# Attention and SwiGLU on one core: where buffers begin, when the next batch is loaded, and where attention products stand

## The chip, the core and the metric

The kernel runs on one core of one Trainium2 chip. The core has a matrix engine (PE, with its weight loads shown as PEld), a vector engine (DVE), a scalar engine (ACT), GpSimd (POOL) and SP, which here only issues DMAs. The metric is the device time of one execution in microseconds. The kernel before was run three times: 1498.76, 1501.85 and 1501.93 us, median 1501.85. A further execution was taken with the profiler.

## What is computed

Two stages follow one another, for four batches of 12416 tokens with 128 channels:

```python
h = mab(I, x)                      # 32 inducing rows attend to all tokens of a batch
a = mab(x, h)                      # each token attends to the 32 rows of h
g, val = a @ w_gate, a @ w_val     # 128 -> 1536
out = (g / (1 + exp(-g)) * val) @ w_out    # 1536 -> 128

def mab(q, kv):
    s = scale * (q @ kv.T); s = exp(s - s.max(-1)); return (s / (s.sum(-1) + 1e-9)) @ kv
```

All inputs and the output are float32, and the large products are made from a rounded part (`hi`) and a remainder (`lo`).

## The kernel before

**Columns, tiles and slots.** The tokens of a batch are cut into 25 columns. The first has 512 tokens, the next twelve have 512 each, the last twelve 480 each. A column is worked through in 12 tiles of the hidden width, so a batch has 300 slots, 12 to a column. In each slot `front` makes two products from the buffer `stack` of the column (gate, L668, and value, L669), ACT computes silu (L671) and DVE the product h (L676). One slot later `split` rounds h to `h_hi` (L685, mostly ACT) and takes the remainder `h_lo` (L687, POOL, on DVE in three tiles of twelve). Some slots later `back` adds three products to the accumulator of the column (L701 and L702 from `h_hi`, L703 from `h_lo`). The first column of batch 0 has one unsplit product instead (L699). After the twelfth tile, `evac` copies the accumulator to `ob` (L710, DVE) and SP writes it out (L712).

**The order.** It is written out by hand: each engine runs its instructions in the order in which the program issues them. The list `pend` holds split tiles that wait for `back`. `ahead`, the number of tiles in front and pend together, grows by a sixth each slot up to 10 while the attention of the next batch runs, and falls back to 5.

**Attention beside the columns.** While a batch's columns run, the steps of the next batch's attention are issued between `front` and `back`, each from the slot that `plan` gives it: `load_xt` (L225), `s1` and `max_b` (first scores, their maximum), `hacc` (the sum over tokens), `h_c`, `s2` (second scores), `exp2`, and `proj_round` (the weights `tw` of the batch). `PA` holds the slots for batch 1 (beside batch 0), `PB` those for batches 2 and 3. `clear` moves a step off the slots that `TABU` bars (slot 5 of each column, in `PA` only). The steps s1, max_b, hacc, h_c and s2 take a buffer of `ps_o`, which has two and also holds the column's accumulator.

**From attention to a column.** `post` makes the next group of columns from the second scores: sum, reciprocal and norm, transpose `aT`, then `a_hi` (L457, a copy on DVE that rounds; once on ACT at the start), `a_lo` (L462, POOL) and `spread` (L478), whose DMAs copy both into `stack`, 12 slots apart for each column.

**Loads.** The buffers `xt_sb` are four. Batch 0 reads its last four chunks of x from them by slots 50, 54, 60 and 66, and the loads of batch 1 go into the same buffers in that order. SP issues its DMAs in the order of the program, and one that has to wait for its buffer holds all that come after it.

**Where buffers begin.** The pools lie one behind another in each partition. Adding up their tiles, the three `stack` buffers begin at 160 bytes modulo 256, the eleven `h_hi` and ten `h_lo` at 32, and the weights that these products load (`tw`, `wo_hi`, `wo_lo`) at 224. A buffer of 512 columns has 2048 bytes, so all of a pool begin alike.

Of the kernel before, what the change touches and what calls it, by code (L numbers as in the profile page):

```python
# [9 lines left out]
F32 = mybir.dt.float32  # L10
# [22 lines left out]
NF = len(FC)  # L33
W = 32 * max(CH)
WF = 32 * max(FC)
NT = DFF // P
SCALE = 1.0 / math.sqrt(C)

# [62 lines left out]
    70: "sb:84:97:1",  # L101
}

PA = dict(LX=(38, 5), S1=(61, 7), MX=7, E1=10, LN=(27, 4), HA=(3, 3, 3), HB=(9, 6), HC=(8, 4), HD=5, H2=6, E2=5, PR=(0, 3), PQ=2, TABU=(5,))
PB = dict(LX=(0, 9), S1=(25, 7), MX=6, E1=9, LN=(28, 4), HA=(3, 3, 3), HB=(9, 3), HC=(8, 4), HD=6, H2=5, E2=5, PR=(0, 3), PQ=1, TABU=())


@with_exitstack
def induced_set_attention_then_swiglu(ctx: ExitStack, tc: tile.TileContext, xt, xn, ind, wgv, wo, out):
# [52 lines left out]
    class Piece:  # L162
# [23 lines left out]
        def add(self):  # L186
            nc.gpsimd.tensor_add(out=self.w.bitcast(I32), in0=self.t.bitcast(I32), in1=self.lw.bitcast(I32))
# [3 lines left out]

        def lo(self):
            nc.gpsimd.tensor_sub(out=wo_lo[:, self.cs], in0=self.w, in1=wo_hi[:, self.cs].bitcast(F32))

    class Batch:
        pass

    def attention(b, one, xn0=None, xt0=None):
# [253 lines left out]
            st.at[q] = sgl.tile([P, WF], F32, name="aT")  # L452
            nc.vector.transpose(out=st.at[q][:, :32 * FC[q]], in_=sl2(*fblocks(q)).rearrange("p t m -> p (t m)"))

        def a_hi(q, eng=nc.vector.tensor_copy):
            st.ah[q] = sgl.tile([P, WF], F32R, name="a_hi")
            eng(out=st.ah[q][:, :32 * FC[q]], in_=st.at[q][:, :32 * FC[q]])  # L457

# [4 lines left out]

        def stack(u):
            if u not in st.stack:
                st.stack[u] = stp.tile([P, WF], F32R, name="stack")
            return st.stack[u]

        def spread(u):
# [19 lines left out]
            nc.vector.tensor_reduce(out=st.zm, in_=st.zps[:, :M * FC[0]].rearrange("p (t m) -> p t m", m=M), op=ALU.max, axis=AX.X)  # L489

        def z2():
            st.z = att.tile([P, FC[0], M], F32, name="z")
            nc.vector.tensor_sub(out=st.z, in0=st.zps[:, :M * FC[0]].rearrange("p (t m) -> p t m", m=M),
                                 in1=st.zm.unsqueeze(2).broadcast_to([P, FC[0], M]))

# [46 lines left out]
    def plan(st, p):  # L542

        f, s = st.f, []

        def add(slot, step, *args):
            s.append((slot, lambda: f[step](*args)))

        def clear(slot):

            while slot % NT in p["TABU"]:
                slot += 1
            return slot

        def blocks(q):
            return CH0[q], CH0[q] + CH[q]

        for q in range(NCH):
            add(p["LX"][0] + p["LX"][1] * q, "load_xt", q)
            add(clear(p["S1"][0] + p["S1"][1] * q), "s1", q)  # L560
        last = clear(p["S1"][0] + p["S1"][1] * (NCH - 1))
        mb = clear(last + p["MX"])
        add(last + 2, "max_a"), add(mb, "max_b")
        e1 = mb + p["E1"]
        for q in range(NXN):
            add(e1 - p["LN"][0] + p["LN"][1] * q, "load_xn", q)
            add(e1, "exp1_part", q)
            add(e1, "eT", q)
            add(e1 + p["HA"][q], "hacc", q, (0, NXN - 1))
        add(e1, "exp1_part", NXN, NCH - 1)  # L570
        for q in range(NXN, NCH):
            at = clear(e1 + p["HB"][0] + p["HB"][1] * (q - NXN))
            add(at - p["HC"][0], "load_xn", q)
            add(at - p["HC"][1], "eT", q)
            add(at, "hacc", q, (q, q))
        add(at, "h_a")
        add(at + 2, "h_b")
        hn = clear(at + p["HD"])
        add(hn, "h_c")
        for i, q in enumerate(S2O):  # L580
            at = clear(hn + 4 + p["H2"] * i)
            add(at, "s2", *blocks(q))
            if i + NXT < NCH:
                add(at + 1, "load_xt", S2O[i + NXT])
            add(at + 1, "s2_max", *blocks(q))
            add(at + 3, "s2_sub", *blocks(q))
        e2 = at + p["E2"]
        add(e2, "exp2")
        st.e1, st.bursts = e1, {e1, e2}
        for i in range(2):  # L590
            add(e2 + p["PR"][i], "proj_round", i)
            for k in range(NG * NG):
                add(e2 + p["PR"][i] + 3 + k * p["PQ"], "proj_spread", i, k // NG, k % NG)
        for q in range(NF):
            first = [u for u, (p, j) in enumerate(COLS) if p == q][0]
            s += post(st, q, nc.gpsimd, SLOTS + NT * (first - NST) + 2, SLOTS)
        return sorted(s, key=lambda x: x[0])
# [60 lines left out]
    def front(st, b, c, t):  # L658
        u = Tile()
        q, j = COLS[c]  # L660
        u.b, u.q, u.j, u.t = b, q, j, t
        n = u.n = WF if q == 0 else 32 * FC[q]

        u.whole = b == 0 and c == 0
        rhs = st.stack[c][:, :n]
        u.g = ps_gv.tile([P, 512], F32, name="gv")
        u.v = ps_gv.tile([P, 512], F32, name="gv")
        nc.tensor.matmul(out=u.g[:, :n], lhsT=st.w[:, wcol(0, t)], rhs=rhs, start=True, stop=True)  # L668
        nc.tensor.matmul(out=u.v[:, :n], lhsT=st.w[:, wcol(1, t)], rhs=rhs, start=True, stop=True)  # L669
        s = sip.tile([P, WF], F32, name="silu")  # L670
        nc.scalar.activation(out=s[:, :n], in_=u.g[:, :n], func=AF.Silu)  # L671
        if u.whole:
            u.h = hip.tile([P, WF], F32, name="h_hi")
        else:
            u.h = u.v if t in DVE_TILES else hp.tile([P, WF], F32, name="h")
        nc.vector.tensor_mul(out=u.h[:, :n], in0=u.v[:, :n], in1=s[:, :n])  # L676
        return u

    def split(u):
        if u.whole:  # L680
            return
        n = u.n
        u.hi = hip.tile([P, WF], F32R, name="h_hi")
        u.lo = lop.tile([P, WF], F32R, name="h_lo")
        (nc.vector.tensor_copy if u.cast_dve else nc.scalar.copy)(out=u.hi[:, :n], in_=u.h[:, :n])  # L685
        eng = nc.vector if u.t in DVE_TILES or u.last else nc.gpsimd
        eng.tensor_sub(out=u.lo[:, :n], in0=u.h[:, :n], in1=u.hi[:, :n].bitcast(F32))  # L687
# [28 lines left out]
    for b in range(B):  # L716
# [12 lines left out]
        for slot in range(SLOTS):  # L729
            c, t = slot // NT, slot % NT  # L730
            u = front(cur, b, c, t)
            u.cast_dve = t in CAST
            u.last = b == B - 1 and slot == SLOTS - 1
            if wait:
                split(wait[0])
                pend.append(wait.pop(0))
            wait.append(u)
            if slot in bursts:
                u.cast_dve = True
                split(u)  # L740
                pend.append(wait.pop(0))
            for a in (cur, nxt):
                while a is not None and a.steps and a.steps[0][0] <= slot:
                    a.steps.pop(0)[1]()
            ahead = min(ahead + 1 / RAMP, HI) if nxt is not None and slot < last_burst else max(ahead - 1 / RAMP, SKEW)
            if slot in bursts:
                ahead = SKEW
            while len(pend) + len(wait) > ahead:
                back(pend.pop(0))
# [44 lines left out]
```

## Time and profile before

| | |
|---|---|
| three runs | 1498.76, 1501.85, 1501.93 us |
| profiled execution | 1499.66 us, of which the span of the instructions is 1497.6 us |
| granted clock of TensorE | 0.999 |
| PE, PEld busy | 1475.7, 1166.2 us |
| ACT, DVE, POOL busy | 1283.6, 1214.6, 1208.5 us |

The span runs from the first to the last instruction; the few microseconds around it belong to the execution too. Matmul rows give a duration that is modelled and longer than the distance to the next one, so a busy PE has to be read by the distances between starts. "[0.70 <-DVE ob]" in a row is idle time of that engine before it, and what ended it. Idle time is counted from the modelled end.

### The profile page before, as it was taken

How to read it: one execution, taken by the hardware profiler on the slowest of the kernel's cores; microseconds unless marked ns; L12 is line 12 of the kernel's file. 1: busy time of each engine (PE TensorE's matmuls, PEld its weight loads, DVE VectorE, ACT ScalarE, POOL GpSimd, SP SyncE). 2: the span in 40 equal slices, each digit the busy share in tenths (PEclk: the TensorE clock that was granted, in tenths of full speed). 3: DMA queues.
4: the chain of work that ended last, by engine and by line, in shares of the span. 5: the costliest groups of instructions: out<-in, count | busy, mean ns of one | idle time of the engine just before them, and what ended most of it. 6: DMA issues, size and time to landing. Idle time of an engine off the chain costs nothing.

```text
span 1497.6 us, 24960 instructions
## 1 busy us (share of the span) xinstructions
PE 1475.7 (99%) x7465; PEld 1166.2 (78%) x7465; DVE 1214.6 (81%) x2083; ACT 1283.6 (86%) x2389; POOL 1208.5 (81%) x995
## 2 busy tenths in 40 slices
PE   8899999999999999999999999999999999999999
PEld 5576777788887776788887777678888887888887
DVE  6788778878888778788888878878878878878877
ACT  5787888789898887889989888789898898898897
POOL 1588767878898778788888877978889888888887
PEclk9999999999999999999999999999999999999999
DMA  9026322221133333121114324221111111111110
GB/s 369 23 94 187 135 96 94 79 61 56 40 109 120 122 125 112 46 67 37 40 44 131 125 87 156 78 69 48 41 40 35 38 41 41 33 41 39 41 40 20
DMA packets 50822, 119.80 MB, mean 80 GB/s; under 512 B 11392, under 2 KB 28288, under 8 KB 50688
## 3 DMA queue, kind: packets, MB, share of 16 engines
q1 hardware_dynamic: 50688, 118.22, 24.6%
q8 instruction: 59, 0.97, 0.3%
q14 instruction: 75, 0.61, 0.1%
HBM read 62.87 MB, written 25.43 MB: 59 GB/s over the span
## 4 chain that ended last, share of the span: by engine, by line
PE 87%; POOL 2%; ACT 2%; DVE 1%; issue 1%; DVEq 0%; ACTq 0%; POOLq 0%
PE o L701 17%; PE o L703 17%; PE o L702 16%; PE gv L668 16%; PE gv L669 16%; PE o L257 2%; POOL h_lo L687 2%; PE o L305 1%; ACT h_hi L685 1%; ACT silu L671 1%; POOL s_all L449 1%; DVE h L676 1%; PE gv L406 0%; ACT s_all L289 0%; DVE ob L710 0%
## 5 line engine op out<-in xcount | busy, mean ns | idle before, releaser
L687 POOL TENSOR_TENSOR h_lo<-h,h_hi 128x512 fp32r<-128x512 f32 (+1 forms) x890 | 1109.5, 1270 | 238.8 <-ACT h_hi L685 186.9
L671 ACT ACTIVATE silu<-gv 128x512 f32<-128x512 f32 (+1 forms) x1200 | 704.4, 588 | 127.0 <-PE gv L668 89.6
L676 DVE TENSOR_TENSOR h<-gv,silu 128x512 f32<-128x512 f32 (+1 forms) x891 | 594.3, 668 | 206.8 <-ACT silu L671 162.3
L685 ACT CAST h_hi<-h 128x512 fp32r<-128x512 f32 (+1 forms) x788 | 475.5, 603 | 54.0 <-DVE h L676 47.6
L668 PE MATMUL gv<-stack,tw 128*128 128x512 f32 (+1 forms) x1200 | 469.3, 391 | 1.3 <-ACT h_hi L685 0.8
L701 PE MATMUL o<-h_hi,wo_lo 128*128 128x512 f32 (+1 forms) x1188 | 464.4, 391 | 3.8 <-DVE ob L710 2.1
L703 PE MATMUL o<-h_lo,wo_hi 128*128 128x512 f32 (+1 forms) x1188 | 463.2, 390 | 0.6
L669 PE MATMUL gv<-stack,tw 128*128 128x512 f32 (+1 forms) x1200 | 461.8, 385 | 1.8 <-DVE h L676 0.6
L702 PE MATMUL o<-h_hi,wo_hi 128*128 128x512 f32 (+1 forms) x1188 | 458.5, 386 | 0.0
L701 PEld LDWEIGHTS o<-h_hi,wo_lo 128*128 128x128 f32 x1188 | 223.0, 188 | 81.9 <-issue 33.9
L669 PEld LDWEIGHTS gv<-stack,tw 128*128 128x128 f32 x1200 | 225.2, 188 | 53.9 <-ACT silu L671 4.8
L668 PEld LDWEIGHTS gv<-stack,tw 128*128 128x128 f32 x1200 | 225.7, 188 | 50.2 <-issue 3.8
L703 PEld LDWEIGHTS o<-h_lo,wo_hi 128*128 128x128 f32 x1188 | 222.4, 187 | 52.6 <-POOL h_lo L687 12.1
L702 PEld LDWEIGHTS o<-h_hi,wo_hi 128*128 128x128 f32 x1188 | 223.2, 188 | 36.8
L676 DVE TENSOR_TENSOR gv<-gv,silu 128x512 f32<-128x512 f32 (+1 forms) x297 | 201.7, 679 | 46.4 <-ACT silu L671 40.7
L687 DVE TENSOR_TENSOR h_lo<-gv,h_hi 128x512 fp32r<-128x512 f32 (+1 forms) x297 | 197.3, 664 | 1.0
L685 ACT CAST h_hi<-gv 128x512 fp32r<-128x512 f32 (+1 forms) x294 | 167.9, 571 | 4.8 <-DVE gv L676 2.5
L710 DVE COPY ob<-o 128x512 f32<-128x512 f32 (+1 forms) x100 | 66.3, 663 | 1.4 <-PE o L703 1.4
L685 DVE CAST h_hi<-h 128x512 fp32r<-128x512 f32 (+1 forms) x103 | 46.1, 448 | 0.0
L462 POOL TENSOR_TENSOR a_lo<-aT,a_hi 128x512 fp32r<-128x512 f32 (+2 forms) x27 | 36.2, 1340 | 1.5 <-ACT a_hi L457 1.5
L433 POOL TENSOR_TENSOR s_all<-s_all,mx 128x448 f32<-128x448 f32 (+3 forms) x28 | 26.9, 961 | 0.7 <-DVE mx L429 0.7
L449 POOL TENSOR_TENSOR s_all<-s_all,sm 128x512 f32<-128x512 f32 (+2 forms) x27 | 25.9, 958 | 0.4 <-DVE sm L445 0.4
(159 smaller groups left out, 497.4 us busy)
## 6 DMA issues: line engine op xcount, KB each, us to landing
xt_sb<-xt SPq DMA_DIRECT2D x32, 896.0 KB, 5.1
xn_sb<-xn SPq DMA_DIRECT2D x18, 896.0 KB, 6.2
out<-ob SPq DMA_DIRECT2D x52, 256.0 KB, 2.0
out<-ob SPq DMA_DIRECT2D x48, 240.0 KB, 2.0
stack<-a_hi SPq DMA_DIRECT2D x96, 64.0 KB, 2.0
stack<-a_lo SPq DMA_DIRECT2D x96, 64.0 KB, 2.0
stack<-a_hi SPq DMA_DIRECT2D x96, 60.0 KB, 2.0
stack<-a_lo SPq DMA_DIRECT2D x96, 60.0 KB, 2.0
```

Source lines behind the costliest of these rows:

```text
L449: eng.tensor_mul(out=a, in0=a, in1=st.sm[q][:, :FC[q]].unsqueeze(2).broadcast_to([P, FC[q], M]))
L462: eng.tensor_sub(out=st.al[q][:, :n], in0=st.at[q][:, :n], in1=st.ah[q][:, :n].bitcast(F32))
L668: nc.tensor.matmul(out=u.g[:, :n], lhsT=st.w[:, wcol(0, t)], rhs=rhs, start=True, stop=True)
L669: nc.tensor.matmul(out=u.v[:, :n], lhsT=st.w[:, wcol(1, t)], rhs=rhs, start=True, stop=True)
L671: nc.scalar.activation(out=s[:, :n], in_=u.g[:, :n], func=AF.Silu)
L676: nc.vector.tensor_mul(out=u.h[:, :n], in0=u.v[:, :n], in1=s[:, :n])
L685: (nc.vector.tensor_copy if u.cast_dve else nc.scalar.copy)(out=u.hi[:, :n], in_=u.h[:, :n])
L687: eng.tensor_sub(out=u.lo[:, :n], in0=u.h[:, :n], in1=u.hi[:, :n].bitcast(F32))
L701: nc.tensor.matmul(out=o[:, :n], lhsT=wo_lo[:, ws], rhs=u.hi[:, :n], start=(t == 0), stop=False)
L702: nc.tensor.matmul(out=o[:, :n], lhsT=wo_hi[:, ws], rhs=u.hi[:, :n], start=False, stop=False)
L703: nc.tensor.matmul(out=o[:, :n], lhsT=wo_hi[:, ws], rhs=u.lo[:, :n], start=False, stop=(t == NT - 1))
L710: nc.vector.tensor_copy(out=ob[:, :n], in_=o[:, :n])
```

## The change

Four things are changed.

1. The buffers of the pools `stp`, `hip` and `lop` get 64 more columns (`WB`), 2304 bytes, so that a column can begin at an offset in them. `AT` gives the offsets in columns of stack, h_hi and h_lo: 16, 48 and 48 for columns of 512 tokens (so 160 + 64 and 32 + 192 bytes, both 224 modulo 256), none for those of 480. The tile z of the start moves from the pool `att` (two buffers) to `sgl` (one), which makes the space. The net shift of the pools behind is a multiple of 256 bytes.
2. The loads of x for batch 1 are issued from slot 51 on, every fifth slot, where they began at 38.
3. `TABU` and `clear` are gone. Instead a step that takes a buffer of `ps_o` is held back, with all steps of its list behind it, while the tile that `back` takes next is the last or the first of a column.
4. `a_hi` in `post` is made by a reduction (maximum over one element) on DVE, where it was a copy.
The start still makes its one a_hi on ACT.

```diff
+WB = WF + 64
+AT = (16, 48, 48), (0, 0, 0)
...
-PA = dict(LX=(38, 5), S1=(61, 7), MX=7, E1=10, LN=(27, 4), HA=(3, 3, 3), HB=(9, 6), HC=(8, 4), HD=5, H2=6, E2=5, PR=(0, 3), PQ=2, TABU=(5,))
-PB = dict(LX=(0, 9), S1=(25, 7), MX=6, E1=9, LN=(28, 4), HA=(3, 3, 3), HB=(9, 3), HC=(8, 4), HD=6, H2=5, E2=5, PR=(0, 3), PQ=1, TABU=())
+PA = dict(LX=(51, 5), S1=(61, 7), MX=7, E1=10, LN=(27, 4), HA=(3, 3, 3), HB=(9, 6), HC=(8, 4), HD=5, H2=6, E2=5, PR=(0, 3), PQ=2)
+PB = dict(LX=(0, 9), S1=(25, 7), MX=6, E1=9, LN=(28, 4), HA=(3, 3, 3), HB=(9, 3), HC=(8, 4), HD=6, H2=5, E2=5, PR=(0, 3), PQ=1)
...
+    def at(u):
+
+        return AT[u > NG * FC.count(max(FC))]
...
-        def a_hi(q, eng=nc.vector.tensor_copy):
+        def same(out, in_):
+            nc.vector.tensor_reduce(out=out, in_=in_.unsqueeze(2), op=ALU.max, axis=AX.X)
+
+        def a_hi(q, eng=same):
...
-                st.stack[u] = stp.tile([P, WF], F32R, name="stack")
+                st.stack[u] = stp.tile([P, WB], F32R, name="stack")[:, at(u)[0]:][:, :WF]
...
-            st.z = att.tile([P, FC[0], M], F32, name="z")
+            st.z = sgl.tile([P, FC[0], M], F32, name="z")
...
         def add(slot, step, *args):
-            s.append((slot, lambda: f[step](*args)))
-
-        def clear(slot):
-
-            while slot % NT in p["TABU"]:
-                slot += 1
-            return slot
+            def go():
+                f[step](*args)
+
+            go.acc = step in ("s1", "max_b", "hacc", "h_c", "s2")
+            s.append((slot, go))
...
-            u.h = hip.tile([P, WF], F32, name="h_hi")
+            u.h = hip.tile([P, WB], F32, name="h_hi")[:, :WF]
...
-        u.hi = hip.tile([P, WF], F32R, name="h_hi")
-        u.lo = lop.tile([P, WF], F32R, name="h_lo")
+        u.hi = hip.tile([P, WB], F32R, name="h_hi")[:, u.at[1]:u.at[1] + WF]
+        u.lo = lop.tile([P, WB], F32R, name="h_lo")[:, u.at[2]:u.at[2] + WF]
...
             for a in (cur, nxt):
                 while a is not None and a.steps and a.steps[0][0] <= slot:
+
+                    if getattr(a.steps[0][1], "acc", False) and pend and pend[0].t in (NT - 1, 0):
+                        break
                     a.steps.pop(0)[1]()
```

The calls of `clear` in `plan` become their arguments.

More of the change, by code (lines that the diff above doesn't have):

```diff
@@ L559, in plan @@
             add(p["LX"][0] + p["LX"][1] * q, "load_xt", q)
-            add(clear(p["S1"][0] + p["S1"][1] * q), "s1", q)
-        last = clear(p["S1"][0] + p["S1"][1] * (NCH - 1))
-        mb = clear(last + p["MX"])
+            add(p["S1"][0] + p["S1"][1] * q, "s1", q)
+        last = p["S1"][0] + p["S1"][1] * (NCH - 1)
+        mb = last + p["MX"]
         add(last + 2, "max_a"), add(mb, "max_b")
@@ L571, in plan @@
         for q in range(NXN, NCH):
-            at = clear(e1 + p["HB"][0] + p["HB"][1] * (q - NXN))
+            at = e1 + p["HB"][0] + p["HB"][1] * (q - NXN)
             add(at - p["HC"][0], "load_xn", q)
@@ L577, in plan @@
         add(at + 2, "h_b")
-        hn = clear(at + p["HD"])
+        hn = at + p["HD"]
         add(hn, "h_c")
         for i, q in enumerate(S2O):
-            at = clear(hn + 4 + p["H2"] * i)
+            at = hn + 4 + p["H2"] * i
             add(at, "s2", *blocks(q))
@@ L661, in front @@
         u.b, u.q, u.j, u.t = b, q, j, t
+        u.at = at(c)
         n = u.n = WF if q == 0 else 32 * FC[q]
```

## The prediction

> **What bounds the kernel now.** I read the page first, then the groups by form, then the timeline of the matrix engine.
>
> ```profile
> span 1497.6 us, 24960 instructions
> PE 1475.7 (99%) x7465; PEld 1166.2 (78%) x7465; DVE 1214.6 (81%) x2083; ACT 1283.6 (86%) x2389; POOL 1208.5 (81%) x995
> PE 87%; POOL 2%; ACT 2%; DVE 1%; issue 1%; DVEq 0%; ACTq 0%; POOLq 0%
> ```
>
> PE is busy 99% of the span and owns 87% of the chain that ended last: this is a PE-bound kernel, and only two things can make it shorter, less time from one matmul to the next, or fewer moments in which PE waits. The busy time hides both, since a matmul of 0.39 us in the rows is followed by the next one after 0.23. So the distance of starts is what has to be read. Two clean stretches of batch 3, first and last row of each, with the count from the windows view (40 and 43 distances):
>
> ```profile
> 1289.79 0.39 PE L668 MATMUL gv<-stack,tw 128*128 128x512 f32 x1
> ...
> 1298.96 0.39 PE L668 MATMUL gv<-stack,tw 128*128 128x512 f32 x1
> 1379.69 0.38 PE L703 MATMUL o<-h_lo,wo_hi 128*128 128x480 f32 x1
> ...
> 1388.97 0.38 PE L701 MATMUL o<-h_hi,wo_lo 128*128 128x480 f32 x1
> 1290.00:1299.00 9.00, 9.00 (x41) 1.00 0.12 29
> 1380.00:1389.00 9.00, 9.00 (x44) 1.00 0.15 48
> ```
>
> 512 columns: 9.17 / 40 = 229.3 ns a matmul. 480 columns: 9.28 / 43 = 215.8 ns. The 32 columns between them cost 13.5 ns, 0.42 ns each, so 512 columns alone are worth 216 ns and some 13 ns are a fixed part, the same in both widths. The granted clock is 1.00 in both.
>
> **The starts of the buffers.** The 512-column matmuls that stream from the buffers that move:
>
> ```profile
> L668 PE MATMUL gv<-stack,tw 128*128 128x512 f32 x624 | 251.8, 404 | 1.3 <-ACT h_hi L685 0.8 <-DVE h L676 0.3
> L701 PE MATMUL o<-h_hi,wo_lo 128*128 128x512 f32 x612 | 246.1, 402 | 3.8 <-DVE ob L710 2.1 <-DVE hn L311 1.7
> L669 PE MATMUL gv<-stack,tw 128*128 128x512 f32 x624 | 244.1, 391 | 1.8 <-DVE h L676 0.6 <-DVE h_hi L676 0.6 <-ACT silu L671 0.4
> L703 PE MATMUL o<-h_lo,wo_hi 128*128 128x512 f32 x612 | 242.2, 396 | 0.0
> L702 PE MATMUL o<-h_hi,wo_hi 128*128 128x512 f32 x612 | 240.2, 392 | 0.0
> ```
>
> That is 2 x 624 + 3 x 612 = 3084, so each nanosecond of distance is 3.1 us of the kernel: no other part of the change has such a lever. No row shows a start at 224. Low end: the whole fixed part goes, 13 x 3084 = -40 us. High end: the slowest distance that these matmuls keep for a round, in the rows below (three rows are left out, so four distances), 0.96 / 4 = 240 ns, 11 ns more, +33 us.
>
> ```profile
> 1301.26 0.41 PE L668 MATMUL gv<-stack,tw 128*128 128x512 f32 x1
> ...
> 1302.22 0.39 PE L703 MATMUL o<-h_lo,wo_hi 128*128 128x512 f32 x1
> ```
>
> I take zero. The nearest rows are the stretches above: L668 and L669 stream from buffers that begin at 160, L701 to L703 from buffers at 32, and both take 0.23 in the clean rows; and a 480-column stream, which ends half a period further on, has the same fixed part. Two starts and two ends give one price, so a third start most likely gives it again. The Trainium skill, page "SBUF — State Buffer", section "Who interferes with whom", lets only the port pair of VectorE and GpSimd contend and says that PE waits for nobody; by it, too, the term is zero. The same skill's "TensorE: Matmul & The Clock Gate", section "Back-to-back issue gap", has N/2.4 + 2.5 ns, 216 ns at 512 columns; by that the term could reach -41 us, an estimate, and the trace stands 13 ns above it at both widths.
>
> **The rounding of a (L457).**
>
> ```profile
> L457 DVE CAST a_hi<-aT 128x512 fp32r<-128x512 f32 x11 | 12.0, 1091 | 0.0
> L457 DVE CAST a_hi<-aT 128x480 fp32r<-128x480 f32 x12 | 11.1, 928 | 0.0
> L441 DVE TENSOR_REDUCE sm<-s_all 128x16 f32<-128x512 f32 x12 | 8.1, 676 | 0.0
> L441 DVE TENSOR_REDUCE sm<-s_all 128x4 f32<-128x128 f32 x3 | 0.8, 276 | 0.0
> L685 DVE CAST h_hi<-h 128x512 fp32r<-128x512 f32 x55 | 25.4, 464 | 0.0
> 103.30 1.52 DVE L457 CAST a_hi<-aT 128x512 fp32r<-128x512 f32 x1
> 105.02 0.44 PE L668 MATMUL gv<-stack,tw 128*128 128x512 f32 x1
> 106.08 0.50 PE L669 MATMUL gv<-stack,tw 128*128 128x512 f32 x1 [0.62 <-DVE h L676]
> 1361.58 1.23 POOL L687 TENSOR_TENSOR h_lo<-h,h_hi 128x480 fp32r<-128x480 f32 x1 [0.19 <-ACT h_hi L685]
> ```
>
> The same cast takes 464 ns as h_hi and 1091 as a_hi, so some 0.6 us of it is waiting, while POOL runs h_lo back to back. A reduction over one element reads as many elements and writes 512 instead of 16; from 4 to 16 outputs the two L441 rows differ by 400 ns for 384 elements, 1.04 ns each, with nothing left over for 12 more outputs. I take 676 ns. The skill's "VectorE: DVE Perf Modes", section "The perf-mode tier table", speaks against the edit: a 32-bit copy runs at twice the rate of a reduction. By it the 23 casts would grow by 676 - 464 = 0.21 us each, 4.9 us of DVE; the L457 row says that this copy does not get its rate here, and decides.
>
> What PE gains: at 103.30 the long cast holds back DVE's product for h, and PE stands 1.06 instead of 0.23 us between L668 and L669: 1.52 - 0.68 = 0.84 us returns. In the other 22 the shorter cast (0.42 or 0.28 us earlier) reaches PE over ACT and POOL; the POOL row shows 0.19 us of idle behind one of them, while POOL is what PE waits for there. Whether each of the 22 shows it I can't say from one row, so I take half, 22 x 0.19 / 2 = 2.0 us (2.1, rounded down). Ends: 0 (DVE is idle 19% of the span) and 22 x 0.35 = 7.7 us. Together **2.8 us**.
>
> **Loads from slot 51.**
>
> ```profile
> 89.31 23.54 SPq L225 DMA_DIRECT2D xt_sb<-xt  x2
> 121.04 0.58 SPq L478 DMA_DIRECT2D stack<-a_lo  x1
> 123.84 0.40 PE L703 MATMUL o<-h_lo,wo_hi 128*128 128x512 f32 x1
> 125.06 0.47 PE L668 MATMUL gv<-stack,tw 128*128 128x512 f32 x1 [0.82 <-ACT h_hi L685]
> DMA to landing us min/median/max: 3.7/4.4/5.6
> xt_sb<-xt SPq DMA_DIRECT2D x32, 896.0 KB, 5.1
> ```
>
> SP sits on the second load of batch 1 until batch 0 has read that buffer, and behind it wait the output DMA and the spread of column 5 (slot 46). Its last part is issued at 121.04 and lands 3.7 us or more later, at 124.7 (the row of landings is that of these four parts), and slot 60's L668, the first reader, starts at 125.06, 1.22 after L703 instead of 0.23: 0.99 us. The row names ACT, but a wait for several is put down to the last one. With first loads at 51, 56, 61 and 66 the buffers are read out at slots 50, 54, 60 and 66, so SP hardly waits; spread 5 goes out some ten slots before its use. What is late next may be ACT, whose cast the row names; if it ends as late by itself, the gain is gone. The seven loads move together; the first s1 (slot 61) comes ten slots, about 11 us, after its load, and a load lands in 5.1 us. Gain **1.0 us**, ends 0 and 2.0 (later spreads, queued behind the other loads).
>
> **Attention products beside a change of accumulators.** By the slots of the plan and the length of the queue of finished tiles, the new test holds back five steps by one slot: s1 of batch 0, slot 82, and in batches 1 and 2 each s1 at 46 and s2 at 130. Removing the list of barred slots moves one more step, s1 from slot 90 to 89.
>
> ```profile
> 480.01 0.96 PE L257 MATMUL o<-xt_sb,indT 128*32 128x448 f32 x8
> 480.90 0.50 PE L701 MATMUL o<-h_hi,wo_lo 128*128 128x512 f32 x1
> 593.57 0.96 PE L257 MATMUL o<-xt_sb,hTs 128*32 128x448 f32 x8
> 594.50 0.68 DVE L710 COPY ob<-o 128x512 f32<-128x512 f32 x1
> 595.23 0.51 PE L701 MATMUL o<-h_hi,wo_lo 128*128 128x512 f32 x1 [0.70 <-DVE ob L710]
> 157.29 0.50 PE L701 MATMUL o<-h_hi,wo_lo 128*128 128x512 f32 x1 [0.71 <-DVE ob L710]
> PEld o L701 <- DVE ob L710: 6.0, 5, 1.5
> PEld o L305 <- DVE ob L710: 1.9, 3, 0.8
> ```
>
> At 480.01 (slot 46) the product takes the free bank, and L701 follows after 0.89 us. At 593.57 it takes 1.66 us, since the new accumulator wants the bank that ob still reads: 0.77 us lost. The row at 157.29 (slot 82) has the same idle time, and batch 2 the same plan as batch 1: three times 0.77, 2.3 us in all. Held back, the accumulator gets the free bank and the product the late one: it comes one slot later, 3 x 0.23 + 2 x 0.23 = 1.15 us, at 594.72, and ob ends at 595.18. So 0.46 us of the 0.77 stays, as a wait of the product; the L305 row (hacc steps one slot behind a change, which the test doesn't touch) is that wait in the kernel now. Behind the held PE step wait its own steps in the list and, in order, all of PE. Gain 3 x 0.31 = **0.9 us**, ends 0 and 2.3.
>
> The rest costs nothing: z in another pool is used once in the start, and 64 more columns a buffer are address space alone.
>
> **Sum.** 2.8 + 1.0 + 0.9 = 4.7 us off the span of 1497.6. The profiled execution took 1499.66 with what lies around it, so 1495.0; it is 2.2 below the median of the three runs, 1501.85, and against that median I say 1501.85 - 4.7 = **1497.1 us**. What this kernel's measurement tells from no change is about 0.2%, 3 us, so the bounds are 1498.85 and 1504.85.
>
> **Rivals.**
> - *The start matters and 224 is better.* For it: 13 ns of each distance carry no column, and the only streams not yet tried are these. Against it: 160 and 32 are alike. Half of the fixed part, 6.5 x 3084 = 20 us, gives 1477; all of it 1457. ACT and POOL, 86% and 81% busy, leave room for that.
> - *The start matters and 224 is worse* (slower): the weights (tw, wo_hi, wo_lo) also begin at 224 modulo 256, and each weight load starts with the stream before it, so both reads would begin at the same place of the period. At the 240 ns of the slow rows it is 33 us, 1530. It decides from 1.5 ns a matmul (4.7 / 3.084). Against it: no row shows that the two reads disturb each other.
> - *The edits don't reach PE*: POOL stays the late one behind a_hi, spread 5 waits for something else, and the wait for ob moves to the product whole. Gain under 1 us: 1501.
>
> **Chances.** Forecast 0.50 (1494 to 1500), better start 0.24, worse start 0.10, nothing reached 0.16. Faster: 0.43 of the forecast's 0.50, and 0.24, 0.67. Same: 0.07 + 0.15, 0.22. Slower 0.11. The range leaves out the worse start and the far half of the better one: 1476 to 1503.5.
>
> **What would show it.** The starts: two clean stretches at 512 and 480 columns; the 480 one must stay at 215.8, the 512 one tells the first two rivals apart, over or under 229.3 by 1.5 or more. The cast: L457 becomes a reduction near 676 ns and no PE gap of 1.06 us near 105. The loads: no L225 row of SP over 5 us between 90 and 112, and slot 60 without the 0.99. The banks: L701 waits for ob twice instead of five times, and L257 for ob three times near 0.46. I am wrong if 512-column matmuls change their distance at all, or if reduction rows come out over 1.1 us.

## The result and the profile after

The changed kernel took 1488.94 us (median of four runs, 1488.33 to 1489.94) beside 1501.89 us for the kernel before (four runs, 1498.76 to 1502.49). The ratio is 0.9919, with a 95% interval of 0.9901 to 0.9936. That is 13 us less by the medians and 12.2 by the ratio (9.6 to 14.9), where 4.7 had been forecast. The profiled execution took 1488.33 us, and its span went from 1497.6 to 1486.4 us.

In the page of the changed kernel, the span, the busy time of each engine, and the chain that ended last:

```profile
span 1486.4 us, 24961 instructions
PE 1465.9 (99%) x7465; PEld 1166.9 (79%) x7465; DVE 1208.8 (81%) x2083; ACT 1283.6 (86%) x2389; POOL 1205.2 (81%) x995
PE 90%; ACT 3%; DVE 2%; POOL 2%; DMA 2%; issue 1%; SPq 0%; DVEq 0%; ACTq 0%; POOLq 0%
```

PE lost 9.8 us of busy time with the same 7465 matmuls. Busy time counts modelled ends of 0.39 us for matmuls that follow after 0.23, so it covers short pauses too, and the distances have to tell. The lines have moved by eight or so: gate is L676, value L677, the three products of `back` L709 to L711, `a_hi` L462, `ob` L718. In the timeline of PE, the gate's matmul of one slot and that of five slots later, in a column of 512 and in one of 480 (start, duration; five matmuls a slot, so 25 distances):

```profile
1278.47 0.39 PE L676 MATMUL gv<-stack,tw 128*128 128x512 f32 x1
...
1284.13 0.39 PE L676 MATMUL gv<-stack,tw 128*128 128x512 f32 x1
...
1368.97 0.38 PE L676 MATMUL gv<-stack,tw 128*128 128x480 f32 x1
...
1374.38 0.38 PE L676 MATMUL gv<-stack,tw 128*128 128x480 f32 x1
```

512 columns: 5.66 / 25 = 226.4 ns, where they had 229.3. 480 columns: 5.41 / 25 = 216.4, near the 215.8 before (the median of the clean rounds is 216.0 in both traces). The starts are what was changed for the one and not for the other.

The groups by form show the new rounding, and two rows of the timeline the place near 105 us at which PE had stood 1.06 us:

```profile
L462 DVE TENSOR_REDUCE a_hi<-aT 128x480 fp32r<-128x480 f32 x12 | 7.7, 643 | 0.0
L462 DVE TENSOR_REDUCE a_hi<-aT 128x512 fp32r<-128x512 f32 x11 | 7.4, 676 | 0.0
103.74 0.44 PE L676 MATMUL gv<-stack,tw 128*128 128x512 f32 x1
104.02 0.42 PE L677 MATMUL gv<-stack,tw 128*128 128x512 f32 x1
```

643 and 676 ns, and value follows gate after 0.28 us. SP's rows and PE's at slot 60:

```profile
88.06 0.43 SPq L231 DMA_DIRECT2D xt_sb<-xt  x1
...
111.62 4.94 SPq L231 DMA_DIRECT2D xt_sb<-xt  x2
121.67 0.39 PE L711 MATMUL o<-h_lo,wo_hi 128*128 128x512 f32 x1
121.89 0.39 PE L676 MATMUL gv<-stack,tw 128*128 128x512 f32 x1
```

The load that held SP for 23.54 us is gone from 88 us, and slot 60 starts 0.22 us after the matmul ahead of it. In the list of waits (who waits for whom: sum in us, times, longest), first the kernel before, then the changed one:

```profile
PEld o L703 <- POOL h_lo L687: 12.1, 39, 0.5
PE o L701 <- DVE ob L710: 2.1, 3, 0.7
```

```profile
PEld o L711 <- POOL h_lo L695: 5.9, 13, 0.5
PE o L263 <- DVE ob L718: 1.5, 3, 0.6
```

The 39 waits for POOL have become 13. The accumulator (L709) no longer waits for ob; the attention product (L263) does.

### The profile page after: what moved, and what is told of

It reads as the page before. It is cut to its first block, busy times and chain, and to the rows that moved or that the text cites. A ratio compares the mean times of both kernels' runs of the same rounds, so it can differ in the third digit from the quotient of the medians.

```text
span 1486.4 us, 24961 instructions
## 1 busy us (share of the span) xinstructions
PE 1465.9 (99%) x7465; PEld 1166.9 (79%) x7465; DVE 1208.8 (81%) x2083; ACT 1283.6 (86%) x2389; POOL 1205.2 (81%) x995
## 4 chain that ended last, share of the span: by engine, by line
PE 90%; ACT 3%; DVE 2%; POOL 2%; DMA 2%; issue 1%; SPq 0%; DVEq 0%; ACTq 0%; POOLq 0%
PE o L709 17%; PE o L711 17%; PE gv L676 17%; PE gv L677 17%; PE o L710 17%; PE o L263 2%; POOL h_lo L695 1%; PE o L311 1%; ACT silu L679 1%; DMA work<-wgv 1%; DVE h L684 1%; DMA xt<-xt 1%; ACT h_hi L693 1%; PE o L707 1%; POOL s_all L455 0%
## 5 line engine op out<-in xcount | busy, mean ns | idle before, releaser
L695 POOL TENSOR_TENSOR h_lo<-h,h_hi 128x512 fp32r<-128x512 f32 (+1 forms) x890 | 1107.8, 1267 | 232.1 <-ACT h_hi L693 175.3
L676 PE MATMUL gv<-stack,tw 128*128 128x512 f32 (+1 forms) x1200 | 467.7, 390 | 0.7 <-DVE h L684 0.6
L709 PE MATMUL o<-h_hi,wo_lo 128*128 128x512 f32 (+1 forms) x1188 | 463.7, 390 | 1.7 <-DVE hn L317 1.7
L677 PE MATMUL gv<-stack,tw 128*128 128x512 f32 (+1 forms) x1200 | 462.1, 385 | 1.3 <-DVE h_hi L684 0.6
L711 PE MATMUL o<-h_lo,wo_hi 128*128 128x512 f32 (+1 forms) x1188 | 457.9, 385 | 0.6
L709 PEld LDWEIGHTS o<-h_hi,wo_lo 128*128 128x128 f32 x1188 | 223.0, 188 | 78.6 <-issue 37.5
L677 PEld LDWEIGHTS gv<-stack,tw 128*128 128x128 f32 x1200 | 225.0, 187 | 51.1 <-ACT silu L679 5.3
L676 PEld LDWEIGHTS gv<-stack,tw 128*128 128x128 f32 x1200 | 225.5, 188 | 48.6 <-issue 3.0
L711 PEld LDWEIGHTS o<-h_lo,wo_hi 128*128 128x128 f32 x1188 | 222.7, 187 | 46.3 <-POOL h_lo L695 5.9
L718 DVE COPY ob<-o 128x512 f32<-128x512 f32 (+1 forms) x100 | 66.4, 664 | 1.4 <-PE o L711 1.4
```

Source lines behind the costliest of these rows:

```text
L709: nc.tensor.matmul(out=o[:, :n], lhsT=wo_lo[:, ws], rhs=u.hi[:, :n], start=(t == 0), stop=False)
L711: nc.tensor.matmul(out=o[:, :n], lhsT=wo_hi[:, ws], rhs=u.lo[:, :n], start=False, stop=(t == NT - 1))
L718: nc.vector.tensor_copy(out=ob[:, :n], in_=o[:, :n])
```

## The experiments

Each time stands beside runs of the kernel before on the same chip; savings in us are what the ratio leaves to 1, times the median of those (1501.3, 1501.4 and so on), with the ratio's interval.

### The parts alone

**The starts alone** (the kernel before with `WB`, `AT`, `at` and z moved).

```diff
+WB = WF + 64
+AT = (16, 48, 48), (0, 0, 0)
```

> The kernel before with the new buffers and their starts alone (512-column streams at 224 modulo 256, 2304 bytes a buffer, z moved); loads, cast and attention products as before. Theory A, the start makes the stream shorter: 512-column matmuls at 227 ns apart instead of 229.3, 3084 x 2.3 = 7 us, so 1494 to 1495.5; 480-column ones stay at 215.8. Rival B, the gain of the whole change came from the waits (cast, loads, banks) and the shorter distance is only their reflection: 229.3 stays and the time is within 2 us of before.

Measured: 1497.17 us (1495.71 to 1504.21), ratio 0.9974 [0.9961, 0.9988], 3.9 us less (1.8 to 5.9). The distance at 512 columns was that of the changed kernel, 5.67 / 25 = 226.8 ns:

```profile
1233.93 0.39 PE L675 MATMUL gv<-stack,tw 128*128 128x512 f32 x1
...
1239.60 0.39 PE L675 MATMUL gv<-stack,tw 128*128 128x512 f32 x1
```

Its profiled execution took 1504.21 us all the same, the longest of the eight, and it is worth reading. First the windows view behind two places (the figure after the last count is the granted clock, which was 1.00 ahead of both), then rows of the timeline at those places:

```profile
125.00:130.00 5.00, 4.51 (x19) 1.89 (x23) 1.67 (x3) 0.82 (x2) 1.85 (x2) 0.66 0.21 33
600.00:610.00 10.00, 10.00 (x41) 7.21 (x41) 6.88 (x12) 6.21 (x12) 7.29 (x7) 0.83 0.17 48
```

```profile
125.49 0.52 PE L675 MATMUL gv<-stack,tw 128*128 128x512 f32 x1 [2.52 <-DMA stack<-a_lo]
...
595.70 2.68 DVE L463 CAST a_hi<-aT 128x480 fp32r<-128x480 f32 x1
598.30 0.68 DVE L717 COPY ob<-o 128x512 f32<-128x512 f32 x1
...
599.03 0.50 PE L708 MATMUL o<-h_hi,wo_lo 128*128 128x512 f32 x1 [2.88 <-DVE ob L717]
```

Two pauses that the kernel before also has, at slot 60 and at the change of accumulators in batch 1, came out at 2.52 and 2.88 us here, and behind each the granted clock fell: 0.66 and 0.83 are the means of the windows shown, and windows cut to the fall itself (125.77 to 129.18, 600.22 to 603.63) have 0.50 for 3.41 us. The first pause names its cause outright: stack, that is the spread behind the held load. The second is a cast of a_hi that took 2.68 us and kept ob waiting. Both causes are among the edits that this kernel lacks.

**All but the starts** (the changed kernel with all offsets zero, buffers as wide as there).

```diff
-AT = (16, 48, 48), (0, 0, 0)
+AT = (0, 0, 0), (0, 0, 0)
```

> The changed kernel with all offsets zero: 512-column streams begin at 160 (stack) and 32 (h_hi, h_lo) again, but the buffers keep 2304 bytes and lie where the change put them. Theory A (the start modulo 256 is what counts): 229.3 ns between 512-column matmuls and 1488.9 + 7 = about 1496. Rival C (the spacing of the buffers or their new place counts, not the start): 227 ns and about 1489.

Measured: 1493.34 us (1492.05 to 1493.6), ratio 0.9943 [0.9928, 0.9959]. The gate's rows of its timeline, five slots apart:

```profile
1266.06 0.39 PE L676 MATMUL gv<-stack,tw 128*128 128x512 f32 x1
...
1271.79 0.39 PE L676 MATMUL gv<-stack,tw 128*128 128x512 f32 x1
```

5.73 / 25 = 229.2 ns: the old distance, with the new buffers. So it is the start that counts, not the room between the buffers or their new place. That it counts modulo 256 shows here too: the buffers of a pool lie 2304 bytes apart, 2048 in the kernel before, both multiples of 256, and the median round stands at 229.4 ns in both. The changed kernel is 4.4 us below this one (1493.34 - 1488.94).

**The reduction alone.**

```diff
-        def a_hi(q, eng=nc.vector.tensor_copy):
+        def same(out, in_):
+            nc.vector.tensor_reduce(out=out, in_=in_.unsqueeze(2), op=ALU.max, axis=AX.X)
+
+        def a_hi(q, eng=same):
```

> The kernel before with a_hi made by the reduction alone. My prediction: 2.8 us less (0.8 near 105 us, 2.0 over the rest), 1499. Rival: DVE has slack everywhere but near 105 us, 0.8 us less, 1501. L457's row near 676 and 643 ns in both.

Measured: 1495.4 us (1494.87 to 1497.75), ratio 0.9963 [0.9949, 0.9976], 5.6 us less (3.6 to 7.7); the span of the profiled execution is 1492.9, 4.7 below the 1497.6 of the kernel before. Its list of waits has this row:

```profile
PEld o L706 <- POOL h_lo L690: 5.8, 13, 0.5
```

The 39 waits become 13 by this edit alone; the kernels with only the loads or only the held steps changed keep "39". Set against the kernel before slot by slot (starts of the gate's matmuls), the trace gains 0.9 us between slots 40 and 50, where the 1.06 us had been, and after that 0.2 to 0.3 at a time, at 14 or so of the later groups of columns, 3.2 us together. The third place is how long the cast may take. The view of one line gives the shortest, median and longest instruction, in ns: the kernel before, the kernel with the starts alone, and the changed one.

```profile
L457 DVE CAST a_hi<-aT x26: 291/1098/1525, 103.3 to 1411.6; 128x480 fp32r<-128x480 f32 x12, 128x512 fp32r<-128x512 f32 x11, 128x128 fp32r<-128x128 f32 x3
```

```profile
L463 DVE CAST a_hi<-aT x26: 292/1112/2679, 102.0 to 1416.4; 128x480 fp32r<-128x480 f32 x12, 128x512 fp32r<-128x512 f32 x11, 128x128 fp32r<-128x128 f32 x3
```

```profile
L462 DVE TENSOR_REDUCE a_hi<-aT x26: 274/644/677, 102.0 to 1400.7; 128x480 fp32r<-128x480 f32 x12, 128x512 fp32r<-128x512 f32 x11, 128x128 fp32r<-128x128 f32 x3
```

The 26 casts reach 1525 ns in the first and 2679 in the second; the reductions stay at 677 or below. Each kernel has one trace, though. The two others that keep the cast, with the old starts, have 1518 and 1543 ns as their longest, so whether a cast of 2 us belongs to the moved streams or can come in the kernel before as well is not shown.

**The loads alone.**

```diff
-PA = dict(LX=(38, 5), ...
+PA = dict(LX=(51, 5), ...
```

> The kernel before with one edit: the loads of x for batch 1 go out from slot 51 instead of 38. By the prediction SP is free again between 90 and 112, the L478 DMA of column 5 goes out some ten slots before its use, and slot 60 no longer has the 0.99 us: 1.0 us off, about 1500.3 beside a before of 1501.3. Rival 1, spread was not the late one (ACT's cast was): 0. Rival 2, several spreads were late behind the waiting load: up to 2.0 us off. By what the changed kernel without its starts (1493.34) and the reduction alone (1495.4) left between them, 2.1 us are to be shared by this edit and the held-back products.

Measured: 1498.02 us (1496.75 to 1499.06), ratio 0.998 [0.9971, 0.9988], 3.0 us less (1.8 to 4.4). Its slot 60, in the timeline:

```profile
122.43 0.39 PE L703 MATMUL o<-h_lo,wo_hi 128*128 128x512 f32 x1
122.66 0.39 PE L668 MATMUL gv<-stack,tw 128*128 128x512 f32 x1
```

0.23 us: the 0.99 is gone whole, which is the 1.0 us of the forecast, and ACT isn't late behind it. But the runs gain more. In the four traces with the loads at 38, the same place costs 0.99 us (before), 2.7 (starts alone, 125.49 against 122.58), 0.5 (reduction alone, 123.53 against 122.77) and 0.4 (held steps alone, 123.78 against 123.18). The pause varies from kernel to kernel, and at 2.7 us the clock fell behind it.

The trace of this run does not show the other 2 us at slot 60. Slot by slot it gains 1.1 us there and 1.3 ahead of slot 12, where nothing was moved. The 1.3 lie in the start, where the kernel before ran at half clock from 39.06 to 42.47 us and this one did not. Windows of the kernel before, then of a later version with the loads at 51 (all of it moved by 64 bytes, below):

```profile
40.00:60.00 20.00, 16.48 (x50) 8.94 (x48) 16.58 (x26) 16.98 (x31) 9.56 (x8) 0.94 0.02 5
40.00:60.00 20.00, 17.10 (x46) 9.09 (x45) 15.73 (x24) 16.23 (x29) 8.83 (x7) 0.82 0.01 3
```

Ten of the fourteen traces have such a fall of 3.4 us or more that begins between 37 and 39.1 us, eight of those ten with the loads at 51. Over the runs, time goes with the clock: of the 67 runs of the kernel before that stand beside these experiments, the 15 with a mean granted clock of 1.000 took 1497.7 to 1499.4 us and the five at 0.995 took 1503.9 to 1505.8, while all eleven runs with the loads alone had 0.999 or 1.000 and took 1496.8 to 1499.1. Where in those 67 runs the clock fell, at slot 60, in the start or elsewhere, is not on record, so what makes the 3.0 us out of 1.1 stays open.

**The held-back steps alone** (no barred slots, and the test before a step).

```diff
-... PQ=2, TABU=(5,))
+... PQ=2, TABU=())
+            go.acc = step in ("s1", "max_b", "hacc", "h_c", "s2")
...
+                    if getattr(a.steps[0][1], "acc", False) and pend and pend[0].t in (NT - 1, 0):
+                        break
```

> The kernel before with one edit: the list of barred slots is empty and a step that takes a bank of ps_o is held back while the next tile to be added is a first or a last one. By the prediction three moves of 0.77 us of waiting shrink to 0.46: 0.9 us off, about 1500.4 beside a before of 1501.3. Rival 1, the wait moves whole to the held product: 0. Rival 2, nothing of the wait stays: 2.3 us off. The wait rows tell which: L701 for ob twice instead of five times, L257 for ob three times.

Measured: 1499.22 us (1497.58 to 1501.85), ratio 0.9991 [0.9982, 1.0], 1.4 us less (0 to 2.7). The place in batch 1 that the prediction worked through (slot 130), and the wait list:

```profile
592.76 0.39 PE L673 MATMUL gv<-stack,tw 128*128 128x512 f32 x1
593.61 0.96 PE L257 MATMUL o<-xt_sb,hTs 128*32 128x448 f32 x8 [0.45 <-DVE ob L714]
```

```profile
PE o L257 <- DVE ob L714: 1.4, 3, 0.5
```

The held product waits 0.45 us, three times in all, where 0.46 three times was forecast. Slot by slot the trace gains 0.23, 0.25 and 0.22 us at the three places, 0.7 us; 0.9 had been forecast, and the interval reaches down to nothing.

The four parts alone make 3.9 + 5.6 + 3.0 + 1.4 = 13.9 us, the whole change 12.2 by its ratio (9.6 to 14.9): they add up within their intervals.

### What about the start counts

**A start for each column** (the changed kernel; stack, h_hi and h_lo of a column all begin at the same place).

```diff
+SW = [224, 0, 32, 64, 96, 128, 160, 192, 240, 16, 48, 112]
...
+    s = SW[(u - 1) % 12]
+    return (s - 160) % 256 // 4, (s - 32) % 256 // 4, (s - 32) % 256 // 4
```

> The changed kernel with another start for each column, the same for stack, h_hi and h_lo: columns 1 to 12 (512 wide) and 13 to 24 (480 wide) at 224, 0, 32, 64, 96, 128, 160, 192, 240, 16, 48, 112 modulo 256. Theory A1 (the start of the stream by itself counts): one distance for each start, 227 at 224, 229.3 at 32 and 160, others between or beyond; the 480 columns show the same order. Theory A2 (only that stack, h_hi and h_lo begin alike counts, where before they stood 128 bytes apart): 227 in all twelve 512-wide columns. The total says little here.

**The same with the weights moved.** A tile of 64 bytes ahead of them moves the weights to 32 modulo 256; the offsets are worked out anew, so that each column keeps its start.

```diff
+    shift = const.tile([P, 16], F32, name="shift")
+    nc.vector.memset(shift, 0.0)
```

> The sweep of starts again, the same start in each column as in the sweep before, but with everything from the weights on moved by 64 bytes: tw, wo_hi and wo_lo begin at 32 modulo 256 instead of 224. Theory 1, the address of the stream by itself decides: 512 columns keep their least distance (226.6 ns) at 224 and 480 columns theirs (213.4) at 96. Theory 2, what decides is where the stream stands to the weights: the least distances move with them, 512 columns to the start at 32 and 480 columns to the start at 160, and 224 and 96 come out among the others (229 to 234, 216 to 220). The total time says little: about 1499 to 1502 by either, since each start is still used in one column of either width.

Measured: 1500.86 us (one run) and 1501.59 us (1501.03 to 1502.75). With a start for each column the time tells little, the distances tell. 480 columns, gate's rows five slots apart; in the first sweep a column that begins at 96, then one at 192:

```profile
1394.14 0.38 PE L686 MATMUL gv<-stack,tw 128*128 128x480 f32 x1
...
1399.48 0.38 PE L686 MATMUL gv<-stack,tw 128*128 128x480 f32 x1
...
1433.34 0.38 PE L686 MATMUL gv<-stack,tw 128*128 128x480 f32 x1
...
1438.84 0.38 PE L686 MATMUL gv<-stack,tw 128*128 128x480 f32 x1
```

213.6 and 220.0 ns. With the weights moved, the column that begins at 96, then the one at 160:

```profile
1395.72 0.38 PE L688 MATMUL gv<-stack,tw 128*128 128x480 f32 x1
...
1401.17 0.38 PE L688 MATMUL gv<-stack,tw 128*128 128x480 f32 x1
...
1422.12 0.38 PE L688 MATMUL gv<-stack,tw 128*128 128x480 f32 x1
...
1427.45 0.38 PE L688 MATMUL gv<-stack,tw 128*128 128x480 f32 x1
```

218.0 and 213.2 ns: the good start went with the weights, from 96 to 160. The starts of both sweeps that are multiples of 32, by their place behind the start of the weights (ns, the median over clean rounds of five matmuls that lie in one column; first sweep / weights moved):

| start minus weights, modulo 256 | 0 | 32 | 64 | 96 | 128 | 160 | 192 | 224 |
|---|---|---|---|---|---|---|---|---|
| 512 columns | 226.6 / 227.8 | 233.4 / 233.4 | 229.4 / 229.0 | 233.6 / 232.6 | 233.2 / 232.6 | 234.2 / 233.0 | 233.2 / 233.4 | 233.0 / 233.0 |
| 480 columns | 217.4 / 216.0 | 219.8 / 220.0 | 218.2 / 218.2 | 220.0 / 219.8 | 213.4 / 213.4 | 216.8 / 216.8 | 216.0 / 216.0 | 220.0 / 220.0 |

All sixteen pairs agree within 1.4 ns, and most within 0.4; at 512 columns a median rests on some 10 to 15 rounds, which scatter by 0.4 to 5 ns. Of the other four starts (240, 16, 48, 112), only the places 16 and 80 behind the weights come in both sweeps, and they agree as well: 232.2 and 232.1, 231.4 and 231.2 ns at 512 columns. The slowest of all is the place 240, 235.4 ns in the second sweep alone. Halves of 256 are not alike (226.6 at 0, 233.2 at 128).

What counts is where a stream begins against what was moved, and 224 was the best start for 512 columns where the weights begin at 224. The tile of 64 bytes moves the other buffers with the weights. That it is the weights is argued, since they are what these matmuls load beside their streams; weights moved alone were not tried.

**480 columns at 96 throughout.**

```diff
-AT = (16, 48, 48), (0, 0, 0)
+AT = (16, 48, 48), (48, 16, 16)
```

> The changed kernel with offsets for the 480-column buffers too: 48, 16 and 16 columns, so that stack, h_hi and h_lo all begin at 96 modulo 256 there. By the sweep of starts, where 480 columns at 96 kept 213.4 ns against 216.0 now, 2.6 ns x 2880 matmuls = 7.5 us come off the changed kernel: about 1481.4 beside its 1488.9. Rival: the sweep's one column was undisturbed by its neighbours and the other engines take up the slack: 0 to 4 us, 1485 or more, with distances near 213.4 in clean rounds all the same. If the distance itself stays near 216, the sweep's reading by column was wrong.

Measured: 1495.46 us (1493.09 to 1496.35), ratio 0.9963 [0.9948, 0.9977]: 6.5 us *above* the changed kernel. The column that kept 213.6 ns in the sweep, and one further on, here:

```profile
1388.34 0.38 PE L676 MATMUL gv<-stack,tw 128*128 128x480 f32 x1
...
1393.84 0.38 PE L676 MATMUL gv<-stack,tw 128*128 128x480 f32 x1
...
1427.88 0.38 PE L676 MATMUL gv<-stack,tw 128*128 128x480 f32 x1
...
1433.32 0.38 PE L676 MATMUL gv<-stack,tw 128*128 128x480 f32 x1
```

220.0 ns, then 217.6 (a cycle of rounds of 1087, 1091 and 1089 ns) with the same starts and the same weights; between the two lies one pause. So the start alone does not fix the distance: something is carried from matmul to matmul, and there are several values in which a round can stay. That misses what was expected, and it says that a column in a sweep need not tell what a whole kernel with that start does.

**Pairs** (stack, h_hi and h_lo with starts of their own, another set for every six columns).

```diff
+PAIRS = ((16, 240, 240), (160, 96, 96)), ((48, 16, 16), (96, 32, 32)), ((96, 160, 160), (224, 96, 96)), ((32, 96, 96), (96, 224, 224))
+WIDE = ((32, 32, 32), (96, 32, 32)), ((224, 224, 32), (224, 32, 224)), ((224, 96, 96), (32, 224, 224)), ((224, 32, 32), (160, 224, 224))
```

> The changed kernel with a pair of starts for every six columns: one for stack, one for h_hi, one for h_lo. What is open: 480 columns at 96 kept 213.4 ns in one column of the sweep, but 220 or 217.8 when all their columns begin there, so the start alone does not fix the distance. Theory 1, each matmul has the distance of its own stream's start and the round of five is their weighted mean: 512 columns with stack at 224 and h_hi, h_lo at 32 give (2 x 226.6 + 3 x 229.4) / 5 = 228.3, with stack at 160 and the others at 224 (2 x 233.2 + 3 x 226.6) / 5 = 229.2. Theory 2, a phase is carried from matmul to matmul and the whole round locks to one value: rounds away from those means by over 1 ns, several values for one pair, and steps of some 6.7 ns in the sum of a round. If a pair holds the 480 columns under 215 ns through all its six columns, also after their pauses, it is worth up to 2.6 x 2880 = 7.5 us; 16 with 240 and 48 with 16 stood at 214.4 and 214.7 in the mixed rounds of the sweep.

Measured: 1499.59 us (1498.24 to 1500.96). 512 columns with stack at 224 and the others at 32:

```profile
1227.98 0.40 PE L680 MATMUL gv<-stack,tw 128*128 128x512 f32 x1
...
1233.78 0.40 PE L680 MATMUL gv<-stack,tw 128*128 128x512 f32 x1
```

232.0 ns, not the weighted mean of 228.3; with stack at 160 and the others at 224 rounds stayed at 231.4 or 234.0, not 229.2. Theory 1 falls. Of the eight pairs for 480 columns, 48 with 16 kept 214.6 to 214.8 ns in 58 of 65 clean rounds, 16 with 240 stood at 214.3 in about one half of its rounds and mostly at 217.7 in the other, and the other six have medians of 216.0 to 218.6. Most values that last lie in steps: a round of five takes 1067, 1073, 1080, 1087, 1093 or 1100 ns at 480 columns, 1133, 1147, 1153, 1160 or 1167 at 512, that is multiples of some 6.7 ns. Rounds of 1083 and 1117 ns, half a step between, last too, in fewer columns.

**Pairs 32 bytes apart** (stack 32 bytes behind h_hi and h_lo, twelve places of four columns).

```diff
+BACK = (0, 32, 48), (64, 80, 96), (112, 128, 160), (192, 208, 224)
...
+        s = BACK[b][(u - 13) // 4]
```

> The changed kernel with twelve pairs for the 480 columns, four columns each: h_hi and h_lo at s, stack 32 bytes further on, s from 0 to 224. If it is the distance of 32 between the two that makes 48 and 16 good, most of the twelve stay under 215 ns. If the place to the weights counts as well (a phase that both set), they range from 214 to 220 as in the first sweep and 48 with 16 is one of few.

Measured: 1492.82 us (1491.92 to 1493.15). None of the twelve stayed under 215 ns (medians 216.0 to 218.6, and 223.2 at 80). So the 32 bytes aren't the reason either; the place to the weights counts as well. A rule that gives the good pairs was not found.

### A version that beats both

**480 columns at 48 and 16.**

```diff
-AT = (16, 48, 48), (0, 0, 0)
+AT = (16, 48, 48), (36, 60, 60)
```

> The changed kernel with stack at 48 and h_hi, h_lo at 16 modulo 256 in the 480-column columns (offsets 36, 60, 60), the pair that kept 214.6 to 214.8 ns through six columns of batch 1. If the pair keeps it in all four batches: 216.0 - 214.7 = 1.3 ns x 2880 = 3.8 us off the changed kernel, 1485 beside its 1488.9. Rival: after other pauses and other neighbours the rounds lock to another value, as 96 did (213.4 in one column, 220 when used throughout): no gain or a loss, 1488 to 1495, with rounds of 480 columns spread over several values.

Measured: 1484.94 us (1484.36 to 1485.35), ratio 0.989 [0.9866, 0.9913]. 1485 had been expected. Gate's rows of batch 3:

```profile
1418.03 0.38 PE L676 MATMUL gv<-stack,tw 128*128 128x480 f32 x1
...
1423.39 0.38 PE L676 MATMUL gv<-stack,tw 128*128 128x480 f32 x1
```

214.4 ns, and the rounds come back to that value after each pause, in all four batches. The time is 4.0 us below the changed kernel, but the two stood beside different runs, and the intervals of their ratios overlap (0.9866 to 0.9913 against 0.9901 to 0.9936). The traces decide: slot by slot the four stretches of 480 columns are 1.2, 1.0, 1.1 and 1.1 us shorter than in the changed kernel, 4.4 in all, where 3.8 had been forecast.

**All of it moved by 64 bytes**, weights and streams together, with no offset changed.

```diff
+    shift = const.tile([P, 16], F32, name="shift")
+    nc.vector.memset(shift, 0.0)
```

> The kernel with 480 columns at 48 and 16, with everything from the weights on moved by 64 bytes and no offset changed: the weights begin at 32 modulo 256, 512 columns at 32, 480 columns at 112 (stack) and 80 (h_hi, h_lo). The readings by column misled once (96 throughout), so the theory is put to a whole kernel. Theory 2, what counts is where streams stand to the weights: the distances stay at 226.6 and 214.7 ns and the time at 1485. Theory 1, the addresses by themselves count: 32 and 112 with 80 were none of the good ones, about 229.4 and 217.4 ns, so 2.8 x 3084 + 2.7 x 2880 = 16 us slower at most, 1493 to 1501.

Measured: 1486.62 us (1484.62 to 1487.62), ratio 0.9896 [0.9879, 0.9912]. First a 512 column, then a 480 one:

```profile
1261.36 0.39 PE L678 MATMUL gv<-stack,tw 128*128 128x512 f32 x1
...
1267.03 0.39 PE L678 MATMUL gv<-stack,tw 128*128 128x512 f32 x1
...
1420.48 0.38 PE L678 MATMUL gv<-stack,tw 128*128 128x480 f32 x1
...
1425.84 0.38 PE L678 MATMUL gv<-stack,tw 128*128 128x480 f32 x1
```

226.8 and 214.4 ns, as before the move, where theory 1 wanted 229.4 and 217.4. For a whole kernel, too, it is the place to the weights, and to what moves with them, that counts, not the address by itself. The trace is 2.5 us longer than that of the version above; 1.8 of it lie ahead of slot 12, where the clock is at one half for 6.8 us from 37.1 us and for 3.4 us from 50.75 (the second of the windows shown for the loads).

## Why the prediction was right, and where it was wrong

The measured 1488.94 us lies in the stated range, 1476 to 1503.5, because the range had been drawn out for a better start. The forecast's own stretch, 1494 to 1500, missed it, and the sign that the prediction gave for being wrong, 512-column matmuls that change their distance at all, came.

**The starts: wrong.** The step that failed is "I take zero", and its reason "two starts and two ends give one price, so a third start most likely gives it again". The two starts had never been seen apart: stack at 160 and h_hi, h_lo at 32 share one round, and a round has one value. Taken apart in the sweep, 160 keeps 233.2 ns and 32 keeps 229.4. The row was right, but it was one observation and not two. By the runs the starts are worth 3.9 us (1.8 to 5.9). The Trainium skill, page "SBUF — State Buffer", section "Who interferes with whom", by which PE waits for nobody, had been read as backing for the zero; the runs show a PE whose matmuls change their distance by up to 7.6 ns (226.6 to 234.2 in the table) with no other engine's work changed. The skill's "TensorE: Matmul & The Clock Gate", section "Back-to-back issue gap", gives 216 ns at 512 columns as the gap of single matmuls; no start that was tried kept less than 226.6.

The rival *224 is better* had the mechanism and the sign, and missed the size, 20 us. Its distance fell by 2.8 ns and not by half of the 13. And not all of 2.8 x 3084 = 8.6 us arrived: by the starts of the gate's matmul at the slots where the 512 columns begin and end, the profile with the offsets gains 0.5 (from slot 30 on), 1.0, 1.0 and 1.6 us in the four batches over the one without, 4.1 in all. After each pause the rounds stand at some 231 ns for one to three rounds before they come back to 226.6, and beside attention such pauses are frequent; batch 3, which has none beside it, gets most. The rival *224 is worse* took the common start with the weights for a harm. By the sweeps it is the other way: that common start is what is good about 224.

**The rounding: mechanism right, size too small.** The duration held (643 and 676 ns against 676), and so did the 0.84 us near 105 us (0.9 in the trace). The term of the other 22, 2.0 us, was mis-sized: half of them had been taken, eleven, at 0.19 us each, and the trace gains 3.2 us in 14 steps of 0.13 to 0.32, while 26 waits for POOL are gone. The runs give 5.6 us for the edit (3.6 to 7.7). What makes up the rest is not shown. Casts of 2 us and more would, but of the four traces with the cast only that of the starts alone has them. The Trainium skill's "VectorE: DVE Perf Modes", section "The perf-mode tier table", would have had the edit cost 4.9 us of DVE, by the prediction's estimate; instead a_hi went from 23.1 to 15.1 us (12.0 + 11.1 against 7.7 + 7.4).

**The loads: right in the trace, too small in the runs.** The pause of 0.99 us at slot 60 is gone whole, and the later trace names the spread as its cause, as argued from the SP rows against the releaser that the page had named. But 0.99 was one value of a pause that cost 0.4 to 2.7 us in four traces. The runs give 3.0 us (1.8 to 4.4), of which the trace shows 1.1 at slot 60; falls of the clock, which weren't in the sum, may be the rest, but no run shows where.

**The held-back products: right.** 0.9 us forecast, 0.7 in the trace, 1.4 (0 to 2.7) in the runs; what stays is 0.45 us three times. Only L709 was to wait for ob twice and waits no more.

**The base of the sum.** The forecast took 4.7 us off the median, 1501.85, with terms from an execution of 1499.66. No run shows what set that median 2.2 us above the profile. The clock has a part in such differences: the profile before has the fall in the start and that of the changed kernel has none, and 1.3 of the 11.2 us between their spans lie ahead of slot 12. The changed kernel spread less, 1.6 us between its runs, where the kernel before has 3.7 in the runs beside it and 8.2 in all. It does not hold for each kernel with these edits: the last version above spreads by 3.0 us, with two of its four runs at a clock of 0.996.

So the sign and the order of the three small terms came from the profile as argued. What lay between 4.7 and the 12.2 that the ratio gives is the starts (3.9 us by their own runs, taken as zero), the rounding (5.6 for 2.8), the loads (3.0 for 1.0) and the held products (1.4 for 0.9), less 1.7 by which the parts alone exceed the whole.

## What to carry to other kernels

Where a kernel is bound by matmuls that follow one another without a pause, read the distance of their starts and compare it between streams, and try where the streams begin against where the weights begin, in a whole kernel and not only in a column: it moved 512-column matmuls between 226.6 and 234.2 ns here, for nothing but an offset. Two buffers that are used in the same round are one observation, not two. And a pause read from one profile is one value: the same place cost 0.4 to 2.7 us in four traces here. Compare the clock in the start as well, before a difference of 1 us between two traces is put down to an edit.

## What was not expected of the hardware

- The distance of matmuls depends on where the stream begins against the weights (or what moved with them), modulo 256 bytes, and on what went before: with the same addresses, 480 columns stayed at 213.4, 217.7 or 220.0 ns for whole columns, and a pause could change one for another. Most lasting values of a round lie some 6.7 ns apart. What inside the chip makes this was not shown, nor why 48 with 16 comes back after a pause and 96 doesn't.
- Behind pauses of PE of 2.5 and 2.9 us the granted clock stood at one half for 3.41 us. In the start, all fourteen traces have a pause of 1.6 us near 38 us, and ten have such a fall there (one of them for 6.8 us), so the length of that pause alone doesn't decide it. Slot 12 began at 60.8 to 61.5 us in the four without the fall and at 61.7 to 63.7 in the ten with it. What decides was not tried.
- The same cast on DVE took 464 ns on the mean as h_hi (408 to 1478) and up to 2679 ns as a_hi; the reduction over one element, with the same input and output as a_hi, never took more than 680 in the ten traces that have it. That POOL's work beside it makes the cast long is argued from the rows, not tried apart.
